# A transformer block on one core: two weight slabs get their own place, some scalings may run on GpSimd, and the instruction order is planned anew

## The chip, the core and the metric

One core of one Trainium2 chip runs the whole kernel. The core has a matrix engine (TensorE, PE in the profile), a vector engine (VectorE, DVE), a scalar engine (ScalarE, ACT), a general engine (GpSimd, POOL) and a synchronising engine (SyncE, SP), which here only issues DMA transfers. Each engine runs its own list of instructions in order; semaphores hold an instruction back until what it needs is there. The metric is the device time of one launch in microseconds (us). Before the change it is 1142.18 us, the median of three runs (1142.15 to 1142.33).

## What is computed

The input is x with 2048 tokens of 1024 numbers, in bfloat16. A conditioning vector c gives six vectors of 1024 numbers: `mod = silu(c) @ w_mod`, split into sa, ca, ga, sb, cb, gb.

1. `h = layernorm(x) * (1 + ca) + sa`, then attention with 32 heads of width 32. The heads have their own queries (`h @ wq`) but share one key (`h @ wk`) and one value (`h @ wv`). Then `x = x + ga * (attention @ wo)`.
2. `h = layernorm(x) * (1 + cb) + sb`, then a gated feed-forward layer of inner width 3584: `silu(h @ w1) * (h @ w3)`, times w2. Then `x = x + gb * (that)`.

## The kernel before

**Work.** The 2048 tokens are eight blocks of 256. Keys and values are made for all tokens at the start. Then attention goes block by block: for each block eight groups of four heads, and for each group eight *steps*. In a step (`s_exp`, line 834) PE computes the scores of 256 keys against 256 queries for four heads (8 matmuls with 32 rows each, into tile S), and ACT takes the exponential of them in two instructions of 128x1024 (into tile U). There are 512 steps in all, 64 for each block, numbered here 0 to 511. The feed-forward work of block n runs between the steps of block n+1: the projection by wo and the second layer norm (`wo`, line 928), 14 slabs of w1 and w3 (`slab`, line 985: 32 matmuls of 256 columns each), and four quarters of w2 (`quarter`, line 1022: 56 such matmuls). The last block's feed-forward work has nothing beside it and forms a tail. Besides these, `av` (line 865) computes probabilities times values and, with the sums of pairs that DVE makes (`pairs`, line 854, tile PS), the softmax denominators.

**Setup.** At the start x arrives in pieces; each tile of 128 tokens is normalised (`lnt1`, line 640: statistics on DVE, the reciprocal root on POOL, the normalising on ACT or DVE), transposed on PE into HT, and copied out of the PSUM buffer by ACT or DVE. `mod_cols` (line 673) computes sa and ca from two pieces of w_mod for each; `scale0` (line 689) multiplies the first 256 columns of wq by (1 + ca), in eight instructions that may run on DVE or POOL. The first step needs sa, because the key and query biases come from it (`k_bias`, line 703). The other four vectors come from `mod_chunk` (line 793), whose weights go through two places called WMB, inside the tile W2S.

**Second norm.** For blocks 1 to 6 the normalised tokens are transposed by two DMA transfers, and eight DVE instructions of 128x256 (one for each 128 features, cc = 0 to 7) multiply by (1 + cb) and add sb. PE's first slab matmuls read these pieces in the order of cc.

**Weight slabs.** Each slab of w1 and w3 (two transfers of 512 KB, `slab_dma`, line 970) goes to one of three places in turn: two in W13, where wq lies until the last query projection has read it, and one in HT, where the transposed tokens lie until then. W2S holds two quarters of w2; before that it holds x tiles 6 to 15 and the WMB places.

**Order.** No order is written out by hand. A planner (`Placer`, line 194) runs when the kernel is built. Every operation has a duration that the planner is told, a due time `vt`, and an engine or a choice of engines. `choose` (line 284) takes, among the operations that could start about now, the one with the least due time. `PLAN` (line 115) has an entry for every 16 steps: how far from the earliest start it may look, some switches, and an offset of the due time for each kind of operation and engine ("slab/pe": -74). Another PLAN therefore gives another order on each engine. POOL operations are given a longer duration where the planner believes that DVE holds them up. In the profile all recorded instructions have line 22, so they are told apart by tiles.

Of the kernel before, what the change touches and what calls it, by code (L numbers as in the profile page):

```python
# [6 lines left out]
ALU = mybir.AluOpType  # L7
# [35 lines left out]
class Graph:  # L43
# [63 lines left out]
    def alias(self, new, old):  # L107
# [5 lines left out]


PLAN = [
    (0.0, 0.12, 0.2, 1, 0.7,
     {"wo/pe": -19, "mc/pe": 25, "slab/dve": -28, "ln/dve": -40, "k/pe": 5, "mod/pe": 114, "mc/dve": 1}),
    (0.0, 0.12, 0.1, 1, 1.3, {"mc/pe": 27, "q/dve": -2, "ln/pe": 6, "ln/act": 32, "v/pe": 15, "mod/pe": 18}),
    (0.0, 0.12, 0.1, 1, 0.9,
     {"mc/pe": 27, "slab/act": -5, "q/dve": -2, "ln/pe": 6, "ln/act": 32, "v/pe": 15, "mod/pe": 18}),  # L120
    (0.0, 0.12, 0.1, 1, 0.9,
     {"q/pe": -119, "mc/pe": 27, "slab/act": -5, "q/dve": -2, "ln/pe": 6, "ln/act": 32, "v/pe": 15, "mod/pe": 18,
      "kb/pe": -44, "mc/dve": -51}),
    (0.0, 0.16, 0.2, 1, 2.6,
     {"slab/pe": -74, "q/pe": 2, "av/dve": 20, "slab/dve": 32, "slab/act": -7, "q/dve": -2, "mc/dve": 6}),
    (0.0, 0.16, 0.2, 1, 1.6,
     {"slab/pe": -74, "q/pe": 2, "av/dve": 20, "slab/dve": 32, "slab/act": -7, "q/dve": -2, "mc/dve": 6}),
    (0.0, 0.16, 0.2, 1, 1.3,
     {"slab/pe": -74, "q/pe": 2, "av/dve": 20, "slab/dve": 32, "slab/act": -7, "q/dve": -2, "mc/dve": 6}),
    (0.0, 0.13, 0.2, 1, 1.3,  # L130
     {"slab/pe": -74, "q/pe": 2, "av/dve": 20, "slab/dve": 32, "slab/act": -7, "wo/dve": 106, "q/dve": -2,
      "mc/dve": 6}),
    (0.0, 0.13, 0.2, 1, 1.3,
     {"slab/pe": -74, "q/pe": 2, "pair/dve": 22, "av/dve": 20, "slab/dve": 49, "slab/act": -7, "wo/dve": 106,
      "q/dve": -2, "mc/dve": 6}),
    (0.0, 0.11, 0.0, 1, 2.4, {"wo/pe": 4, "slab/pe": 107, "quarter/pe": -2, "q/pe": -26, "an/dve": 4, "q/dve": -119}),
    (0.0, 0.11, 0.02, 1, 2.6,
     {"wo/pe": 4, "slab/pe": 107, "quarter/pe": -2, "q/pe": -26, "an/dve": 4, "q/dve": -119}),
    (0.0, 0.11, 0.02, 1, 2.6,
     {"wo/pe": 4, "slab/pe": 107, "quarter/pe": -2, "q/pe": -26, "an/dve": 4, "q/dve": -119}),  # L140
    (0.0, 0.11, 0.2, 1, 2.6,
     {"wo/pe": 135, "quarter/pe": 20, "mc/pe": -8, "pair/dve": 119, "av/dve": -14, "an/dve": 72,
      "quarter/dve": -26, "wo/dve": 65, "q/dve": -66}),
    (0.0, 0.11, 0.2, 1, 1.4, {"wo/pe": -20, "slab/pe": 107, "q/pe": -26, "an/dve": 54, "q/dve": -119}),
    (0.0, 0.11, 0.02, 1, 3.1,
     {"wo/pe": -20, "q/pe": -26, "mc/pe": -3, "av/dve": 8, "an/dve": 54, "slab/dve": 29, "q/dve": -119}),
    (0.0, 0.11, 0.05, 0, 2.3,
     {"av/pe": -15, "q/pe": -9, "mc/pe": 109, "pair/dve": -1, "an/dve": 4, "slab/act": 15, "q/dve": 7,
      "mc/dve": 6}),
    (0.0, 0.11, 0.2, 1, 2.4,  # L150
     {"wo/pe": 17, "quarter/pe": -15, "mc/pe": -8, "pair/dve": -39, "av/dve": 1, "an/dve": 72,
      "quarter/dve": -26, "wo/dve": 65, "q/dve": -72}),
    (0.0, 0.12, 0.2, 1, 1.3, {"slab/pe": -12, "av/dve": 57}),
    (0.0, 0.11, 0.2, 1, 2.9,
     {"av/pe": -12, "wo/pe": -19, "slab/pe": -9, "quarter/pe": -39, "pair/dve": -2, "an/dve": -117,
      "quarter/dve": -16, "q/dve": -105}),
    (0.0, 0.11, 0.2, 1, 1.9,
     {"av/pe": -12, "wo/pe": -19, "slab/pe": -9, "quarter/pe": -39, "pair/dve": -2, "an/dve": -117,
      "quarter/dve": -16, "q/dve": -105}),
    (0.0, 0.11, 0.2, 1, 1.9,  # L160
     {"av/pe": -12, "wo/pe": -19, "slab/pe": -9, "quarter/pe": -39, "pair/dve": -2, "an/dve": -117,
      "quarter/dve": -16, "q/dve": -105}),
    (0.0, 0.11, 0.2, 0, 0.7,
     {"av/pe": -12, "wo/pe": -19, "slab/pe": -9, "quarter/pe": -39, "pair/dve": -2, "an/dve": -143,
      "quarter/dve": -16, "q/dve": -105}),
    (0.0, 0.11, 0.05, 1, 3.1,
     {"wo/pe": -17, "mc/pe": -8, "av/dve": 1, "an/dve": 47, "slab/act": 11, "quarter/dve": -26, "wo/dve": 86}),
    (0.0, 0.11, 0.05, 1, 3.1,
     {"wo/pe": -17, "mc/pe": -8, "av/dve": 1, "an/dve": 47, "slab/act": 11, "quarter/dve": -26, "wo/dve": 86}),
    (0.0, 0.11, 0.05, 1, 3.1,  # L170
     {"wo/pe": -17, "mc/pe": -8, "av/dve": 1, "an/dve": 47, "slab/act": 11, "quarter/dve": -26, "wo/dve": 86}),
    (0.0, 0.14, 0.2, 0, 0.1, {"slab/pe": -12, "pair/dve": -20, "av/dve": -18, "slab/dve": -24}),
    (0.0, 0.11, 0.05, 0, 3.3,
     {"wo/pe": -17, "mc/pe": -8, "pair/dve": 43, "av/dve": 14, "slab/act": 9, "quarter/dve": -26}),
    (0.0, 0.11, 0.05, 0, 3.3,
     {"wo/pe": -17, "mc/pe": -8, "pair/dve": 43, "av/dve": 14, "slab/act": 9, "quarter/dve": -26}),
    (0.0, 0.11, 0.2, 1, 1.4,
     {"av/pe": -15, "quarter/pe": -3, "q/pe": -9, "mc/pe": 33, "pair/dve": -16, "av/dve": -5, "an/dve": 18,
      "quarter/dve": -37, "q/dve": 7, "mc/dve": 6}),
    (0.0, 0.11, 0.2, 1, 1.4,  # L180
     {"quarter/pe": -3, "q/pe": -9, "mc/pe": 33, "av/dve": -5, "an/dve": 18, "quarter/dve": 74, "q/dve": 7,
      "mc/dve": 6}),
    (0.0, 0.11, 0.0, 1, 1.4,
     {"quarter/pe": -3, "q/pe": -9, "mc/pe": 33, "av/dve": -5, "an/dve": 18, "quarter/dve": 74, "q/dve": 7,
      "mc/dve": 6}),
    (0.0, 0.11, 0.05, 0, 4.1,
     {"wo/pe": -17, "slab/pe": -70, "mc/pe": -8, "pair/dve": 43, "av/dve": 14, "slab/dve": 97, "slab/act": 9,
      "quarter/dve": -26}),
    (0.0, 0.11, 0.2, 0, 3.3,
     {"slab/pe": -13, "quarter/pe": 27, "mc/pe": 61, "slab/dve": -16, "quarter/dve": 6, "wo/dve": 2}),  # L190
]


# [257 lines left out]
def build(nc, x_in, wq_in, wk_in, wv_in, wo_in, w1_in, w3_in, w2_in, c_in, wmod_in, out, S, D, F):  # L451
    G = Graph(nc)
    op = G.op
    NC = D // P
# [72 lines left out]
    O2B = HTf[:, o:o + 1024].rearrange("p (s t d) -> p s t d", s=2, t=2)  # L527
    o += 1024
    assert o <= NC * S
    W13SL = [W13[:, 0], W13[:, 1], W13C]  # L530
    WQ = W13[:].rearrange("p a b c f -> p (a b c f)").rearrange("p (c f) -> p c f", c=NC)
    WM0 = Uf[:, 0:NC * 2048].rearrange("p (c f) -> p c f", c=NC)
    WMB = [W2f[:, 10 * D:10 * D + NC * 512].rearrange("p (c f) -> p c f", c=NC),
# [52 lines left out]
        dma("sp", dst, x2[tt0 * P:(tt0 + cnt) * P, :].rearrange("(t p) d -> p t d", p=P), ("XL", tt0),  # L586
            cnt * P * D * 2, writes=keys, vt=vt, bw=FAST)

    WSPL = (0, 4, NC)

    def wm_dma(fld, h, vt):
        c0, c1 = WSPL[h:h + 2]
# [326 lines left out]
    def h2t(n):  # L919
        return H20 if n == 0 else QT[:, n - 1, :, :]  # L920

    def h2k(n):
        return [("H20", cc) for cc in range(NC)] if n == 0 else [("QT", n - 1, cc) for cc in range(NC)]

    def xk(n, t, qs=range(4)):
        return [("X", n % NX, t, q) for q in qs]

    def wo(n, vt):
        G.tag = "wo"
        for t in range(2):  # L930
# [26 lines left out]
        for hh in range(2):  # L957
            s = Sess()
# [4 lines left out]
            for k in range(4):  # L963
# [21 lines left out]
    def slab(n, s, vt):  # L985
        G.tag = "slab"
        slab_dma(n, s, vt - 12)
        r = (n * NSLAB + s) % NW
        g = (n * NSLAB + s) % 2
        ss = [Sess(), Sess()]  # L990
        for m in range(2):
# [213 lines left out]
```

## Time and profile before

| what | value |
|---|---|
| median of 3 runs | 1142.18 us (1142.15 to 1142.33) |
| profiled execution, its own time | 1142.53 us |
| its span (first to last instruction) | 1140.7 us |
| granted TensorE clock | 1.00 |
| PE busy, matmul instructions | 1115.7 us, 15538 |
| ACT busy | 1024.3 us |
| DVE busy | 953.9 us |
| POOL busy | 38.3 us |
| first matmul of step 0 | 30.49 us |
| first matmul of step 511 | 1041.95 us |

Times within the profile count from the start of the span. A busy PE is not the same as a PE at its best: matmuls overlap, and the profile models their ends. The starts of the instructions are what the readings below use. A step's time is the time from the first score matmul of a step to that of the next.

### The profile page before, as it was taken

What the parts mean: (1) busy time and instruction counts of PE and PEld (TensorE: products, weight loads), DVE (VectorE), ACT (ScalarE), POOL (GpSimd) and SP (SyncE); (2) the same over time, 40 slices, a digit from 0 to 9 for tenths busy, and PEclk for the clock granted to TensorE, in tenths of its full rate; (3) what the DMA queues carried; (4) which work ended last, traced back from release to release, by engine and by line L of the source; (5) the groups of instructions that cost most, each with busy time, mean ns of one, the idle gap of its engine ahead of it and who ended that gap; (6) DMA issues with size and microseconds to landing.
All of it is one profiled execution on the core that took longest, in us unless ns stands there. A gap on an engine that the chain in (4) does not pass through costs nothing.

```text
span 1140.7 us, 34695 instructions
## 1 busy us (share of the span) xinstructions
PE 1115.7 (98%) x15538; PEld 756.8 (66%) x15568; DVE 953.9 (84%) x1557; ACT 1024.3 (90%) x1161; POOL 38.3 (3%) x83
## 2 busy tenths in 40 slices
PE   8999999999999999999999999999999999999998
PEld 7644556666577756776567656776577656776887
DVE  7888899998888888888979799888978988888442
ACT  5999999999999999999999999999999999996110
POOL 4100000000000000000000010000100000000000
PEclk9999999999999999999999999999999999999999
DMA  9500379665596668665696659675686658667793
GB/s 345 179 2 1 113 222 245 181 187 155 132 264 194 172 163 221 191 196 154 145 253 196 173 143 236 192 204 131 156 249 192 174 140 231 194 188 202 222 291 118
DMA packets 374291, 209.45 MB, mean 184 GB/s; under 512 B 17536, under 2 KB 365952, under 8 KB 374144
## 3 DMA queue, kind: packets, MB, share of 16 engines
q1 hardware_dynamic: 373712, 207.11, 65.2%
q8 instruction: 122, 2.00, 0.8%
q14 instruction: 25, 0.20, 0.1%
q10 hardware_dynamic: 432, 0.13, 0.0%
HBM read 199.89 MB, written 4.19 MB: 179 GB/s over the span
## 4 chain that ended last, share of the span: by engine, by line
ACT 48%; PE 41%; DVE 8%; DMA 2%; issue 1%; SPq 0%; POOL 0%; DVEq 0%
ACT U L22 44%; PE PB L22 29%; PE S L22 12%; DVE PS L22 4%; ACT HT L22 4%; DVE QT L22 1%; DMA W<-in_A_wq_dram 1%; DVE HT L22 1%; DVE RB L22 1%; DVE X L22 0%; DMA QT<-XNB 0%; SPq L22 0%; DVE ST L22 0%; DVE XNB L22 0%; DVE RC L22 0%
## 5 line engine op out<-in xcount | busy, mean ns | idle before, releaser
L22 ACT ACTIVATE U<-S 128x1024 bf16<-128x1024 f32 x1024 | 962.8, 1105 | 15.7 <-PE S L22 7.7
L22 DVE TENSOR_TENSOR PS<-U 128x2048 bf16<-128x2048 bf16 x256 | 309.1, 1213 | 21.3 <-ACT U L22 19.2
L22 DVE TENSOR_TENSOR PS<-PS 128x1024 bf16<-128x1024 bf16 x368 | 248.9, 685 | 4.0
L22 PE MATMUL PB<-QT,W 128*128 128x256 bf16 x1856 | 230.6, 273 | 0.9 <-DVE RB L22 0.4
L22 PE MATMUL S<-QT,KT 32*128 32x256 bf16 x4096 | 203.4, 273 | 7.8 <-ACT U L22 5.5
L22 PEld LDWEIGHTS PB<-QT,W 128*128 128x128 bf16 x1856 | 169.9, 98 | 49.3 <-issue 26.8
L22 PE MATMUL PB<-W2S,HT 128*128 128x256 bf16 x1512 | 189.8, 273 | 0.0
L22 PEld LDWEIGHTS PB<-W2S,HT 128*128 128x128 bf16 x1512 | 136.9, 98 | 43.8 <-issue 27.2
L22 PEld LDWEIGHTS S<-QT,KT 32*128 32x128 bf16 x4096 | 60.7, 92 | 134.8 <-ACT U L22 122.4
L22 PE MATMUL PB<-U,V 128*32 128x256 bf16 x4032 | 125.6, 273 | 1.6 <-DVE HT L22 1.0
L22 PE MATMUL PB<-QT,HT 128*128 128x256 bf16 x960 | 120.6, 273 | 0.6 <-DVE HT L22 0.3
L22 PEld LDWEIGHTS PB<-U,V 128*32 128x32 bf16 x4032 | 99.7, 96 | 23.4 <-issue 10.8
L22 ACT ACTIVATE HT<-PB 128x512 bf16<-128x512 f32 (+1 forms) x110 | 76.4, 696 | 32.7 <-PE PB L22 32.6
L22 PEld LDWEIGHTS PB<-QT,HT 128*128 128x128 bf16 x960 | 87.7, 98 | 25.8 <-issue 14.0
L22 PE MATMUL PB<-HT,W 128*128 128x256 bf16 (+1 forms) x561 | 98.5, 316 | 2.4 <-issue 1.6
L22 DVE SCALAR_TENSOR_TENSOR HT<-HT,PB 128x512 bf16<-128x512 bf16 x102 | 69.4, 681 | 31.8 <-ACT HT L22 30.9
L22 DVE TENSOR_TENSOR HT<-HT,PB 128x512 bf16<-128x512 bf16 x102 | 69.5, 682 | 15.0 <-PE PB L22 13.2
L22 PEld LDWEIGHTS PB<-HT,W 128*128 128x128 bf16 x576 | 50.2, 97 | 37.0 <-issue 13.9
L22 PE MATMUL PB<-WO,QT 128*128 128x512 bf16 x217 | 54.0, 380 | 1.8 <-issue 1.3
L22 DVE STREAM_TRANSPOSE RB<-PB 128x256 f32<-128x256 f32 x63 | 28.2, 447 | 29.6 <-PE PB L22 29.4
L22 POOL TENSOR_SCALAR RS<-MV 128x1 f32<-128x1 f32 x32 | 11.3, 354 | 1015.4 <-DVE MV L22 1010.4
L22 DVE COPY RB<-PB 128x256 f32<-128x256 f32 x63 | 26.4, 419 | 18.5 <-PE PB L22 18.5
(112 smaller groups left out, 648.9 us busy)
## 6 DMA issues: line engine op xcount, KB each, us to landing
W<-in_B_w_dram SPq DMA_DIRECT2D x150, 512.0 KB, 4.9
W2S<-in_B_w_dram SPq DMA_DIRECT2D x28, 1792.0 KB, 8.3
HT<-in_B_w_dram SPq DMA_DIRECT2D x74, 512.0 KB, 4.9
W2S<-in_w_mod_dram SPq DMA_DIRECT2D x8, 1024.0 KB, 6.8
X<-in_A_x_dram SPq DMA_DIRECT2D x8, 512.0 KB, 6.3
U<-in_w_mod_dram SPq DMA_DIRECT2D x4, 1024.0 KB, 11.4
out_dram<-X SPq DMA_DIRECT2D x7, 512.0 KB, 7.9
U<-in_B_w_dram SPq DMA_DIRECT2D x1, 3584.0 KB, 14.0
```

Source lines behind the costliest of these rows:

```text
L22: return getattr(e, call[0])(*call[1], **call[2])
```

## The change

Four things are changed in the text of the kernel.

- Slabs 0 and 1 of block 0 get places of their own (numbers 3 and 4) inside W2S: slab 0 where x tiles 10 to 13 lay, slab 1 where x tiles 6 to 9 and then one WMB place lay. All other slabs keep the place that they had. The first two quarters of w2 now must wait until these slabs have been read.
- Each vector of w_mod that `mod_cols` needs is loaded as 6 and 2 pieces of the inner dimension in place of 4 and 4.
- The second norm's scaling of blocks 1 to 6 is planned with 0.258 us in place of 0.17, and may be placed on POOL, with 0.8 us.
- PLAN has other entries, so that all engines' orders can differ everywhere.

```diff
 PLAN = [
-    (0.0, 0.12, 0.2, 1, 0.7,
-     {"wo/pe": -19, "mc/pe": 25, "slab/dve": -28, "ln/dve": -40, "k/pe": 5, "mod/pe": 114, "mc/dve": 1}),
...
+    (0.0, 0.2, 0.2, 0, 1.3, {"mc/pe": -16, "pair/dve": -90, "av/dve": -32, "k/pe": -82, "k/dve": 48, "mod/pe": 53}),
+    (0.0, 0.16, 0.2, 1, 1.5,
+     {"mc/pe": 77, "pair/dve": -90, "q/dve": -23, "ln/pe": -133, "k/pe": -188, "k/dve": 48, "v/pe": 86,
+      "mod/pe": 53, "kb/pe": 104}),
...
 ]
...
-    W13SL = [W13[:, 0], W13[:, 1], W13C]
+    W13SL = [W13[:, 0], W13[:, 1], W13C] + [
+        W2f[:, k * D:(k + 4) * D].rearrange("p (m c f) -> p m c f", m=2, c=NC) for k in (4, 0)]
+    NE = 2
...
-    WSPL = (0, 4, NC)
+    WSPL = (0, 6, NC)
...
-                   0.17, reads=[("h2r", n, 0), ("h2r", n, 1), ("MODC", 3, cc // 4), ("MODC", 2, cc // 4)],
-                   writes=[h2k(n)[cc]], vt=vt)
+                   0.258, reads=[("h2r", n, 0), ("h2r", n, 1), ("MODC", 3, cc // 4), ("MODC", 2, cc // 4)],
+                   writes=[h2k(n)[cc]], vt=vt, alts=[("pool", lambda cc=cc: [lambda e: e.tensor_scalar(
+                       h2t(n)[:, cc, :], h2t(n)[:, cc, :], MODC[:, 3, cc:cc + 1], MODC[:, 2, cc:cc + 1], ALU.mult,
+                       ALU.add)], 0.8)] if POOLH else [])
...
+    def wslot(n, s):
+        return NW + s if n == 0 and s < NE else (n * NSLAB + s) % NW
+
     def slab_dma(n, s, vt):
-        r = (n * NSLAB + s) % NW
+        r = wslot(n, s)
...
-    G.alias([("W2S", r) for r in range(2)], [("XS", tt) for tt in range(6, NTT)] + [("WMB", 0), ("WMB", 1)])
+    G.alias([("W13", NW, m) for m in range(2)], [("XS", tt) for tt in range(10, 14)])
+    G.alias([("W13", NW + 1, m) for m in range(2)], [("XS", tt) for tt in range(6, 10)] + [("WMB", 1)])
...
+        if n == 0:
+            G.alias([("W2S", r) for r in range(2)], [("XS", tt) for tt in range(6, NTT)] + [("WMB", 0), ("WMB", 1)] +
+                    [("W13", NW + k, m) for k in range(NE) for m in range(2)])
```

The built programs show what the planner makes of it. PE's list has the same 15568 matmuls in both. A matmul list changes its kind (scores; column-tiled av matmuls; all others) 1115 times before and 1102 times after. In the second norm of each of blocks 1 to 6, the pieces cc = 1 and cc = 5 go to POOL and the other six stay on DVE; of the eight scalings in `scale0`, three are on POOL and five on DVE (before two and six).

More of the change, by code (lines that the diff above doesn't have):

```diff
@@ L115 @@
 PLAN = [
-    (0.0, 0.12, 0.2, 1, 0.7,
-     {"wo/pe": -19, "mc/pe": 25, "slab/dve": -28, "ln/dve": -40, "k/pe": 5, "mod/pe": 114, "mc/dve": 1}),
[L118 to L140, printed above, removed]
@@ L141 @@
-    (0.0, 0.11, 0.2, 1, 2.6,
[L142 to L190, printed above, removed]
+    (0.0, 0.2, 0.2, 0, 1.3, {"mc/pe": -16, "pair/dve": -90, "av/dve": -32, "k/pe": -82, "k/dve": 48, "mod/pe": 53}),
+    (0.0, 0.16, 0.2, 1, 1.5,
+     {"mc/pe": 77, "pair/dve": -90, "q/dve": -23, "ln/pe": -133, "k/pe": -188, "k/dve": 48, "v/pe": 86,
+      "mod/pe": 53, "kb/pe": 104}),
@@ new lines @@
+    (0.0, 0.11, 0.2, 0, 2.2,
+     {"wo/pe": 106, "q/pe": -78, "mc/pe": 6, "q/dve": 38, "ln/pe": -118, "ln/dve": 4, "mod/pe": -24}),
+    (0.0, 0.12, 0.2, 0, 0.7, {"wo/pe": 106, "q/pe": -78, "q/dve": 38, "ln/pe": -118, "ln/dve": 4}),
+    (0.2, 0.13, 0.2, 1, 0.8, {"q/pe": 47, "mc/pe": 46, "ln/act": -12, "k/pe": 22}),
+    (0.0, 0.13, 0.2, 1, 1.7, {"q/pe": 47, "mc/pe": 46, "pair/dve": -11, "av/dve": 4, "ln/act": -12, "k/pe": 22}),
+    (0.0, 0.11, 0.2, 1, 1.4, {"q/pe": 47, "mc/pe": 46, "av/dve": 4, "ln/act": -12, "k/pe": 22}),
@@ new lines @@
+    (0.0, 0.11, 0.2, 1, 1.9, {"q/pe": -13, "mc/pe": 46, "av/dve": 4, "ln/act": -12, "k/pe": 22}),
+    (0.0, 0.11, 0.2, 1, 3.9,
+     {"wo/pe": 35, "q/pe": -13, "mc/pe": 46, "av/dve": 4, "slab/dve": 15, "ln/act": -12, "k/pe": 22}),
+    (0.0, 0.11, 0.2, 1, 1.4, {"av/dve": -11, "an/dve": 55, "slab/dve": 1, "q/dve": 9}),
+    (0.0, 0.11, 0.1, 0, 2.4,
+     {"wo/pe": 14, "slab/pe": 12, "quarter/pe": 3, "q/pe": -6, "av/dve": 18, "an/dve": 69, "slab/act": -1,
+      "quarter/dve": -7}),
+    (0.0, 0.11, 0.02, 0, 2.9, {}),
@@ new lines @@
+    (0.0, 0.11, 0.2, 0, 2.9, {"wo/pe": 46, "an/dve": 55, "slab/dve": -89, "q/dve": 67}),
+    (0.0, 0.11, 0.2, 1, 1.3, {"wo/pe": -13, "pair/dve": 6, "an/dve": 55, "slab/dve": -89, "q/dve": 67}),
+    (0.0, 0.11, 0.1, 1, 2.7,
+     {"slab/pe": -132, "q/pe": 47, "mc/pe": 46, "pair/dve": -13, "av/dve": 23, "slab/dve": -39, "slab/act": -20,
+      "quarter/dve": -47, "ln/act": -12, "k/pe": 22}),
+    (0.0, 0.11, 0.1, 1, 2.3,
+     {"slab/pe": -132, "q/pe": 47, "mc/pe": 46, "pair/dve": -13, "av/dve": -84, "slab/act": -20,
+      "quarter/dve": -47, "ln/act": -12, "k/pe": 22}),
@@ new lines @@
+    (0.0, 0.11, 0.2, 1, 4.1,
+     {"wo/pe": 138, "slab/pe": -132, "quarter/pe": 13, "q/pe": 47, "mc/pe": 46, "pair/dve": -13, "av/dve": -83,
+      "slab/dve": -39, "slab/act": -20, "quarter/dve": -47, "ln/act": -12, "k/pe": 22}),
+    (0.0, 0.11, 0.2, 1, 1.3,
+     {"slab/pe": -124, "q/pe": 47, "mc/pe": 46, "pair/dve": -24, "av/dve": -89, "an/dve": -26, "slab/dve": -39,
+      "slab/act": -20, "ln/act": -12, "k/pe": 22}),
+    (0.0, 0.11, 0.05, 1, 3.7,
+     {"wo/pe": -5, "quarter/pe": 48, "pair/dve": -3, "av/dve": -2, "slab/act": -7, "wo/dve": 20}),
@@ new lines @@
+    (0.0, 0.11, 0.05, 1, 3.7,
+     {"wo/pe": -5, "quarter/pe": 48, "pair/dve": -3, "av/dve": -2, "slab/act": -7, "wo/dve": 20}),
+    (0.0, 0.11, 0.2, 1, 2.6,
+     {"wo/pe": 112, "slab/pe": -124, "quarter/pe": 26, "q/pe": 20, "mc/pe": 46, "pair/dve": 13, "av/dve": -89,
+      "an/dve": -26, "slab/dve": -39, "slab/act": -20, "quarter/dve": 35, "wo/dve": -2, "ln/act": -12,
+      "k/pe": 22}),
+    (0.0, 0.11, 0.2, 1, 1.3,
+     {"slab/pe": -124, "quarter/pe": 26, "q/pe": 52, "mc/pe": 46, "pair/dve": 13, "av/dve": -72, "an/dve": -26,
+      "slab/dve": -39, "slab/act": -20, "quarter/dve": 35, "wo/dve": -6, "ln/act": -12, "k/pe": 22}),
@@ new lines @@
+    (0.0, 0.11, 0.05, 1, 2.6,
+     {"slab/pe": -124, "quarter/pe": 26, "q/pe": 20, "mc/pe": 46, "av/dve": -89, "slab/dve": -39,
+      "slab/act": -20, "quarter/dve": 35, "ln/act": -12, "k/pe": 22}),
+    (0.0, 0.11, 0.05, 1, 1.4,
+     {"slab/pe": -124, "quarter/pe": 26, "q/pe": 20, "mc/pe": 5, "av/dve": -89, "slab/act": -20,
+      "quarter/dve": 35, "ln/act": -12, "k/pe": 22}),
+    (0.0, 0.11, 0.2, 0, 1.6, {"wo/pe": 74, "pair/dve": 40, "av/dve": -2, "an/dve": 55, "slab/dve": -102, "q/dve": 6}),
@@ new lines @@
+    (0.0, 0.11, 0.2, 1, 1.4, {"wo/pe": -13, "pair/dve": 40, "av/dve": -2, "an/dve": 55, "slab/dve": -88}),
+    (0.0, 0.11, 0.05, 1, 1.9,
+     {"slab/pe": -124, "quarter/pe": -21, "q/pe": 20, "mc/pe": 46, "pair/dve": 43, "av/dve": -89,
+      "slab/dve": -39, "slab/act": -20, "quarter/dve": 35, "ln/act": -12, "k/pe": 22}),
+    (0.0, 0.11, 0.05, 1, 1.9,
+     {"slab/pe": -124, "quarter/pe": -21, "q/pe": 20, "mc/pe": 46, "pair/dve": 43, "av/dve": -89,
+      "slab/act": -20, "quarter/dve": 35, "ln/act": -12, "k/pe": 22}),
@@ new lines @@
+    (0.0, 0.11, 0.2, 0, 3.4, {"wo/pe": 61, "q/pe": -20, "pair/dve": 3, "slab/dve": -23, "wo/dve": 33}),
+    (0.0, 0.11, 0.2, 1, 1.4, {"wo/pe": -5, "quarter/pe": 48, "pair/dve": -20, "av/dve": -27, "slab/act": -7}),
+    (0.0, 0.11, 0.05, 0, 2.1,
+     {"slab/pe": -124, "quarter/pe": -21, "q/pe": 20, "mc/pe": 46, "pair/dve": 43, "av/dve": -89,
+      "slab/dve": -39, "slab/act": -20, "quarter/dve": 35, "q/dve": -75, "ln/act": -12, "k/pe": 22}),
+    (0.0, 0.11, 0.05, 0, 4.0,
+     {"slab/pe": -124, "quarter/pe": -21, "q/pe": 20, "mc/pe": 46, "pair/dve": 43, "av/dve": -89,
+      "slab/act": -20, "quarter/dve": 35, "q/dve": -75, "ln/act": -12, "k/pe": 22}),
@@ L191 @@
+    (0.0, 0.11, 0.2, 0, 3.7,
+     {"wo/pe": -4, "slab/pe": -43, "q/pe": 20, "mc/pe": 46, "pair/dve": 43, "av/dve": 55, "slab/dve": -39,
+      "slab/act": -20, "quarter/dve": 35, "q/dve": -75, "ln/act": -12, "k/pe": 22}),
 ]
@@ L926, in xk @@
         return [("X", n % NX, t, q) for q in qs]
+    POOLH = True
     def wo(n, vt):
@@ L987, in slab @@
         slab_dma(n, s, vt - 12)
-        r = (n * NSLAB + s) % NW
+        r = wslot(n, s)
         g = (n * NSLAB + s) % 2
```

## The prediction

> **What bounds the kernel now.** I read the page's engine shares first, then the busy time of each stage, then the order of time around single steps.
>
> ```profile
> PE 1115.7 (98%) x15538; PEld 756.8 (66%) x15568; DVE 953.9 (84%) x1557; ACT 1024.3 (90%) x1161; POOL 38.3 (3%) x83
> ACT 48%; PE 41%; DVE 8%; DMA 2%; issue 1%; SPq 0%; POOL 0%; DVEq 0%
> ```
>
> PE and ACT share the chain that ends last. The busy times of the stages, cut at the starts of steps 128, 192, 256 and so on, show why:
>
> ```profile
> 278.50:406.77 128.27, 127.56 (x1807) 86.71 (x1808) 111.14 (x178) 124.79 (x143) 1.91 (x4) 1.00 0.70 188
> 406.77:533.82 127.05, 125.84 (x1790) 85.30 (x1793) 111.31 (x178) 124.99 (x143) 2.74 (x4) 1.00 0.69 187
> 533.82:664.06 130.24, 128.76 (x1808) 86.64 (x1810) 112.03 (x177) 125.14 (x143) 1.91 (x4) 1.00 0.70 189
> 1041.95:1137.54 95.59, 95.54 (x910) 82.25 (x910) 41.47 (x72) 11.06 (x17) 1.58 (x4) 1.00 0.81 228
> ```
>
> The columns are stretch, length, then PE, PEld, DVE, ACT and POOL busy, clock, DMA share and GB/s. With the last stage ACT is done and PE alone works 95 us; so every matmul done earlier shortens the end, and PE's list sets the time. How a step is made up is seen here:
>
> ```profile
> 428.80 0.40 PE L22 MATMUL S<-QT,KT 32*128 32x256 bf16 x8
> 429.13 1.48 PE L22 MATMUL PB<-W2S,HT 128*128 128x256 bf16 x12
> 430.55 0.40 PE L22 MATMUL S<-QT,KT 32*128 32x256 bf16 x8
> ```
>
> From 428.80 to 430.55 a step with 12 matmuls of 256 columns took 1.75 us. A fit over the undisturbed ones of the steps from 120 on gives their prices: scores 0.227, a 256-column matmul 0.108, a 512-column one 0.213, a column-tiled one 0.027, and about 0.115 for each change of kind. With these the 1107 us from step 0 to the last matmul hold 1093 us of PE work and changes of kind and some 14 us of waits. ACT needs 2 x 0.904 a step (0.917 early on), close below.
>
> **Blocks 2 to 7.** PE's order after the change is the same in all six (up to where the last one runs into the tail), and it is the order that block 3 (steps 192 to 255) has now in 62 of 64 steps, block 7 in 61. So they are priced like for like. From step 128 to the last matmul is 859.04 us now (278.50 to 1137.54). Five blocks at block 3's 127.05 and the last one with its tail at 220.26 (917.28 to 1137.54) are 855.51: -3.5 us. Of this 2.3 is PE work that lies earlier or is gone (13 changes of kind fewer, 1.5 us in all), 1.2 are waits.
>
> Block 3 itself contains a wait of 0.65 in step 206 that block 7 has with 0.10 only; there the second DMA transpose came late:
>
> ```profile
> 434.56 2.14 DVE L22 TENSOR_SCALAR QT<-QT,MODC 128x256 bf16<-128x256 bf16 x8 [0.46 <-DMA QT<-XNB]
> ...
> 436.61 0.68 DVE L22 TENSOR_TENSOR HT<-PB,GBR 128x512 bf16<-128x512 f32 x1
> ```
>
> Whether it comes late in all five blocks is open: 0 to -0.5 each, I take -0.25, so -1.2.
>
> **Scalings on POOL.** In six blocks cc = 1 and cc = 5 move from DVE to POOL. The nearest row is the same form, two scalings beside six on DVE:
>
> ```profile
> 17.87 1.95 POOL L22 TENSOR_SCALAR PS<-W,MODC 128x256 bf16<-128x256 bf16 x2 [2.20 <-DMA W<-in_A_wq_dram]
> ...
> 426.95 0.55 POOL L22 TENSOR_SCALAR RS<-MV 128x1 f32<-128x1 f32 x1 [3.43 <-DVE MV L22]
> 427.58 1.40 POOL L22 TENSOR_TENSOR RS<-RS,NH 128x1 f32<-128x1 f32 x1
> ```
>
> That is 0.98 each. DVE's starts there lie 0.42 apart where a POOL instruction begins and 0.20 elsewhere, so each costs DVE 0.22. From DVE's start T, POOL starts 0.14 later and has cc 1 at T+1.2, cc 5 at T+2.2 with its semaphore; DVE ends its six at T+2.0 (now eight at T+2.14). PE needs cc 0 and 1, then 2 and 3, then scores, then 4 and 5. Now the last pair starts at T+2.33 (436.89); afterwards cc 5 at 2.2 and two matmuls of 0.22 give T+2.42. So +0.1 a block, +0.6. Bounds: if the two cost DVE nothing and POOL kept pace, -0.3 a block; if POOL is stretched 2.5-fold, as the second row is (0.57 uncontended, 1.40 beside a DVE pair sum of 1.22), cc 5 comes at T+5.1: +2.9 a block. The first row has this shape and this neighbour, so I stay by it. What DVE saves is 0.1 us, so nothing behind it gains.
>
> **Block 1 (steps 64 to 127).** Its PE work rises by 1.0 us (the earlier work named above). Its waits are 4.1 now, about 2.2 of them where an av group is split over steps; afterwards each group of 64 stands whole in one step, as in block 3, where that costs 0.11. Five of those: -1.7, so -0.7; bounds -2 and +1, and I take -0.5 since ACT is at 124.4 of 124.9 us here.
>
> **The setup.** Here the change costs. The last pieces of sa's weights land at 23.13 and 25.84 now, 1 MB each 2.71. With 6 and 2 parts the first lands at 20.42 + 1.5 x 2.71 = 24.5. And POOL now does three scalings, to 20.8 in place of 19.83, ahead of the roots of tiles 6 and 7, whose transposes PE's list has before all 64 matmuls for sa:
>
> ```profile
> 23.50 2.08 PE L22 MATMUL PB<-SCC,U 128*128 128x64 bf16 x32
> 25.42 0.68 PE L22 MATMUL PB<-IDENT,XNB 128*128 128x128 bf16 x8
> 25.93 2.08 PE L22 MATMUL PB<-SCC,U 128*128 128x64 bf16 x32
> 27.84 0.67 PE L22 MATMUL PB<-IDENT,PS 128*128 128x128 bf16 x8
> 28.35 0.41 PE L22 MATMUL PB<-SAB,PS 128*128 128x64 bf16 x8
> ```
>
> Tile 7 is normalised by 24.7 and transposed by 25.3; 64 matmuls of 0.061 end at 29.2, now 27.84: +1.4. DVE copies two more transposed tiles out (0.6 each) ahead of sa, which it has at about 29.7, now 28.14. I take +1.5 for step 0: 32.0 in place of 30.49. Bounds: by the landing alone 24.5 + 3.9 = 28.4, +0.5; with DVE in full +1.7.
>
> **Block 0 after its first step.** To step 9 ACT sets the pace now: 18 exponentials of 0.917, five copies of 0.92 and one key eviction of 0.48 make 21.6, and the trace has 21.8. Afterwards there are three copies and three evictions: -0.9. DVE gets two copies more and two evictions fewer (1.2 - 0.8), and is busy 3.55 of 4 there: +0.4 if it decides. I take -0.4 in between (-1.1 to +0.6). The rest of the block has the same exponentials and within 0.2 us the same PE work.
>
> **The places of their own.** I cost these at nothing. Slab 0 starts at step 77 (178.0) in both orders; its weights are there at 160.8 already, and what it waits for is the second norm. No wait for a slab transfer is in the table of waits. The new wait, w2's two quarters behind slab 1's last matmul, sits on SP's queue at about 187 in place of 171; behind it are the reloads for slab 5 and on. The two took to 187.1, 16 us; so they end at 203, the first reload at 205 (such landings lie 1.7 apart), slab 5 begins at about 206. The cover is 1 us; without it, each us of lateness is one us, once. The quarters themselves are needed at 250.
>
> **Sum.** -3.5 - 1.2 + 0.6 - 0.5 + 1.5 - 0.4 = -3.5 us. Against the profiled execution (1142.53, span 1140.7) that is 1139.0; the median of the runs lies 0.35 lower: 1138.7 us.
>
> **Rivals.** A measurement of this kernel tells 0.2%, 2.3 us, from no change. (a) No change that counts: the setup's loss stands, and the waits of block 1 and the late transposes stay as they are: -3.5 + 0.6 + 1.0 + 1.5 - 0.4 = -0.8, 1141.4. For it: those gains are my readings of waits, not of work. Against: PE's identical blocks. It decides from 1.2 us of lost gain on. 0.31. (b) Slower: POOL's instruction holds DVE back for its whole 1.0 us, not for 0.22. Then DVE's six end at T+3.6, the last pair starts 1.3 later than now, and six blocks lose 7.6 in place of 0.6: 1145.7. It is slower from 0.95 more a block on. For it: the stretched row at 427.58 shows that the two engines do hinder each other. Against: 17.87 shows 0.22. 0.08. (c) The change of places does what it says: with weights there earlier, block 0's slabs run with no wait at all and the 2.9 us of waits from step 80 to 127 go: 1.2 more than I took, 1137.5; the absence of DMA waits speaks against it. 0.05.
>
> [...]
>
> **Numbers.** My forecast, faster by 1.5 to 6 us, 0.56, of which a tenth falls within 0.2%; (a) 0.31, of which a tenth is slower, with a setup that costs still more; (b) 0.08; (c) 0.05. So faster 0.55, same 0.34, slower 0.11. The range: downward the bounds of block 1 and the transposes (-1.5 and -1.3), not all at once, 1136.0; upward to (a) and the setup's and DVE's upper bounds, 1142.6.
>
> **What would show it.** Step 0 at 32.0; step 128 at 279.1 (278.50 + 1.5 - 0.4 - 0.5); each block from 2 to 6 at 126.5 to 127.2; step 448 at 913.6 (now 917.28). Twelve POOL scalings of 1.0 us. If step 0 is at 31.0 or earlier, the setup is misjudged; if blocks take over 128 us, POOL's scalings are; if slab 5's matmuls wait for DMA, the places are.

## The result, and the profile after

The changed kernel takes 1136.96 us, the median of five runs (1136.06 to 1137.61); five runs of the kernel before beside it took 1142.15 us (1141.78 to 1142.33). The ratio is 0.9955, with a 95% interval of 0.9941 to 0.9970: faster by 5.2 us. The forecast was 1138.7. The profiled execution of the changed kernel took 1137.61 us, with a span of 1135.8; that is 4.9 us less than the one before (1142.53), where the forecast had 3.5 less.

The engine shares and the chain on the page after:

```profile
PE 1117.0 (98%) x15568; PEld 760.0 (67%) x15568; DVE 955.5 (84%) x1546; ACT 1020.8 (90%) x1159; POOL 53.3 (5%) x96
PE 67%; ACT 26%; DVE 4%; DMA 2%; issue 0%; SPq 0%; POOL 0%; DVEq 0%; POOLq 0%
```

PE is as busy as before; of the chain it now holds 67% where it held 41%, and ACT 26% where it held 48%. The stages after, cut at the starts of steps 64, 128, 192, 256, 320 and 511, show where PE stopped waiting. The columns are stretch, length, then PE, PEld, DVE, ACT and POOL busy, clock, DMA share, GB/s; the lines are block 1, blocks 2 to 4, and the last stage:

```profile
156.09:281.41 125.32, 121.30 (x1822) 80.55 (x1823) 114.82 (x189) 124.67 (x143) 2.55 (x4) 1.00 0.70 190
281.41:407.56 126.15, 125.71 (x1792) 85.56 (x1793) 110.72 (x174) 124.79 (x143) 5.03 (x6) 1.00 0.70 189
407.56:534.27 126.71, 125.85 (x1792) 85.40 (x1792) 111.15 (x175) 124.78 (x143) 3.95 (x6) 1.00 0.69 188
534.27:660.42 126.15, 125.70 (x1792) 85.57 (x1792) 111.21 (x175) 124.79 (x143) 5.05 (x6) 1.00 0.70 189
1037.03:1132.51 95.48, 95.48 (x909) 82.21 (x909) 41.13 (x72) 11.06 (x17) 1.59 (x4) 1.00 0.82 228
```

Blocks 2 and 4 to 6 take the same 126.15 us to the hundredth; block 3 is the odd one, with 126.71. The tail is as long as before (95.48; 95.59 in the stage shown before). How a step is made up has not changed: twelve 256-column matmuls stand between scores at 682.46 and 684.20, 1.74 us, where it was 1.75.

```profile
682.46 0.40 PE L22 MATMUL S<-QT,KT 32*128 32x256 bf16 x8
682.79 1.48 PE L22 MATMUL PB<-W2S,HT 128*128 128x256 bf16 x12
684.20 0.40 PE L22 MATMUL S<-QT,KT 32*128 32x256 bf16 x8
```

A fit over the undisturbed steps of the changed kernel gives nearly the prices of the prediction's fit (0.110 us for a 256-column matmul, 0.113 for a change of kind), so these are used for both kernels, and what is left of a step's time beyond them is taken as wait. In the table a length is the time from the first weight load of one step's scores to that of another; PE work is the matmuls and changes of kind in it at those prices, so work and waits are estimates and only the lengths are measured.

| stretch | length before | after | difference | PE work, difference | waits before | after |
|---|---|---|---|---|---|---|
| start to step 0 | 30.49 | 33.29 | +2.80 | | | |
| block 0 | 123.08 | 122.80 | -0.28 | -0.17 | 1.8 | 1.7 |
| block 1 | 124.93 | 125.32 | +0.39 | +0.98 | 4.1 | 3.6 |
| blocks 2 to 6 | 638.78 | 631.31 | -7.47 | -2.31 | 9.1 | 3.9 |
| block 7 to step 511 | 124.67 | 124.31 | -0.36 | 0 | | |
| sum, to step 511 | 1041.95 | 1037.03 | -4.92 | | | |

The setup cost more than forecast (+1.5), block 1 lost 0.4 where 0.5 was to be gained, and blocks 2 to 7 gave more (-7.8 against -4.1 with POOL's part). The second norm that runs in block 3's steps, which the prediction was priced from, reads as follows after, and below it the one in block 5's steps, on DVE and POOL:

```profile
435.28 1.87 DVE L22 TENSOR_SCALAR QT<-QT,MODC 128x256 bf16<-128x256 bf16 x6 [0.40 <-DMA QT<-XNB]
435.35 1.21 POOL L22 TENSOR_SCALAR QT<-QT,MODC 128x256 bf16<-128x256 bf16 x2 [5.59 <-DMA QT<-XNB]
...
686.53 1.22 DVE L22 TENSOR_TENSOR PS<-U 128x2048 bf16<-128x2048 bf16 x1
687.66 1.78 DVE L22 TENSOR_SCALAR QT<-QT,MODC 128x256 bf16<-128x256 bf16 x6
689.36 0.68 DVE L22 TENSOR_TENSOR HT<-PB,GBR 128x512 bf16<-128x512 f32 x1
...
686.55 2.31 POOL L22 TENSOR_SCALAR QT<-QT,MODC 128x256 bf16<-128x256 bf16 x2 [3.92 <-DMA QT<-XNB]
```

DVE's scalings now take 1.78 us where they took 2.14. In block 5 the transposed tokens are there before DVE has finished its pair sum. POOL starts at 686.55, DVE only at 687.66. POOL's first scaling lasts 1.72 us there and its second 0.60; in block 3, where no pair sum runs beside them, the two take 0.6 each. So POOL is held until the pair sum ends, and then both engines are at their scalings at once: eight scalings on DVE alone start 0.257 us apart (2.14 in all, the last one 0.34), six beside POOL's 0.288 (1.78) or 0.306 (1.87). One of POOL's costs DVE 0.08 to 0.12 us. The single instructions of the trace show how: under each of POOL's twelve scalings one on DVE is longer, 0.42 to 0.51 us in place of 0.34, and it ends 0.08 us after POOL's, as if held until then. The next one on DVE begins within 5 ns of POOL's second scaling, takes the usual 0.33 and ends 0.26 before it. So each engine does hold the other up here, but DVE only for the rest of one scaling.

By this reading POOL's 1.72 us beside the pair sum are 1.12 of waiting and its usual 0.60, an estimate from the two durations. For the scalings the trace shows less: one on DVE seems held until POOL is done, but another runs unheld within POOL's 0.60. What makes the difference no run shows.

The wait for POOL's scalings in the setup, first on PE before, then on POOL and PE after, to set beside the rows of the prediction:

```profile
19.97 1.03 PE L22 MATMUL S<-HT,PS 128*128 128x256 bf16 x8 [1.58 <-POOL PS L22]
...
18.21 2.85 POOL L22 TENSOR_SCALAR PS<-W,MODC 128x256 bf16<-128x256 bf16 x3 [1.49 <-DMA W<-in_A_wq_dram]
...
17.36 1.04 PE L22 MATMUL S<-HT,PS 128*128 128x256 bf16 x8
18.23 0.38 PE L22 MATMUL S<-IDENT 128*128 128x256 bf16 x2
21.12 1.39 PE L22 MATMUL S<-HT,PS 128*128 128x256 bf16 x8 [2.50 <-POOL PS L22]
22.30 0.42 PE L22 MATMUL S<-IDENT 128*128 128x256 bf16 x1
22.52 1.06 PE L22 MATMUL S<-IDENT,PS 128*128 128x128 bf16 x8
23.37 2.10 PE L22 MATMUL S<-IDENT 128*128 128x256 bf16 x10
...
26.75 4.04 PE L22 MATMUL PB<-SCC,U 128*128 128x64 bf16 x64
30.63 0.69 PE L22 MATMUL PB<-IDENT,PS 128*128 128x128 bf16 x8
31.15 0.41 PE L22 MATMUL PB<-SAB,PS 128*128 128x64 bf16 x8
```

The ten fillers at 23.37 (IDENT by IDENT, whose result nobody uses) say that something else happens here: 0.21 us each, where in other runs they take 0.12. Two stretches, the second at the half clock and the first as long ahead of it, in the columns of the stages, show what:

```profile
18.27:21.68 3.41, 0.91 (x10) 0.57 (x8) 3.34 (x11) 1.45 (x2) 3.24 (x5) 1.00 1.05 387
21.68:25.09 3.41, 3.41 (x23) 2.63 (x21) 1.92 (x5) 2.48 (x2) 1.68 (x5) 0.50 1.06 383
```

PE was busy for 0.91 of 3.41 us, and then its granted clock was 0.50 for 3.41 us. Before, the wait at this place was 1.58 us and the clock stayed whole. The 64 matmuls for sa begin at 26.75; their second group of 32 began at 25.93 before.

### The profile page after: what moved, and what is told of

It is laid out like the page before. It is cut to its first block, busy times and chain, and to the rows that moved or that the text cites. A ratio compares the mean times of both kernels' runs of the same rounds, so it can differ in the third digit from the quotient of the medians.

```text
span 1135.8 us, 34733 instructions
## 1 busy us (share of the span) xinstructions
PE 1117.0 (98%) x15568; PEld 760.0 (67%) x15568; DVE 955.5 (84%) x1546; ACT 1020.8 (90%) x1159; POOL 53.3 (5%) x96
## 4 chain that ended last, share of the span: by engine, by line
PE 67%; ACT 26%; DVE 4%; DMA 2%; issue 0%; SPq 0%; POOL 0%; DVEq 0%; POOLq 0%
PE PB L22 51%; ACT U L22 25%; PE S L22 16%; DVE PS L22 2%; DMA W<-in_A_wq_dram 1%; ACT HT L22 1%; DVE HT L22 1%; DMA QT<-XNB 0%; DVE X L22 0%; DVE RB L22 0%; SPq L22 0%; DVE QT L22 0%; POOL PS L22 0%; DVE ST L22 0%; DVE XNB L22 0%
## 5 line engine op out<-in xcount | busy, mean ns | idle before, releaser
L22 PE MATMUL PB<-U,V 128*32 128x256 bf16 x4032 | 123.1, 273 | 0.6 <-DVE HT L22 0.6
L22 PE MATMUL PB<-HT,W 128*128 128x256 bf16 (+1 forms) x512 | 93.7, 324 | 0.6 <-DVE HT L22 0.2
L22 PEld LDWEIGHTS PB<-HT,W 128*128 128x128 bf16 x512 | 44.3, 98 | 36.2 <-issue 12.7
L22 PE MATMUL PB<-WO,QT 128*128 128x512 bf16 x232 | 57.3, 381 | 0.0
L22 PEld LDWEIGHTS PB<-WO,QT 128*128 128x128 bf16 x232 | 19.8, 98 | 25.0 <-issue 7.2
```

The lines of the kernel that those rows point to most:

```text
L22: return getattr(e, call[0])(*call[1], **call[2])
```

## The experiments

In every experiment the planner's search is replaced by the recorded list of what it had chosen (operation, engine, PSUM bank), so that one entry can be altered and all else stays:

```diff
-    choose(): least due time among the operations that can start, guided by PLAN
+    run(): the next entry of ORDER
```

The runs fall into three sessions, each with the kernel before on the same chip: 1142.22 us (1141.74 to 1142.47) beside the first four, 1142.44 (1142.03 to 1143.44) beside the next four, 1142.16 (1141.90 to 1142.72) beside the last two. Ratios are to these.

**The old setup with the new order behind it.** My theory was that the setup's loss comes off one for one.

```diff
-ORDER = after
+ORDER = before up to step 0, then after
-    WSPL = (0, 6, NC)
+    WSPL = (0, 4, NC)
```

> The changed kernel, but everything that stood ahead of step 0's scores in the old order is taken from the old kernel (order, engines, the split 4 and 4). Theory A, that the change loses 2.8 us in its setup (step 0 at 33.29 in place of 30.49) and that this loss goes straight to the end: step 0 at 30.5, 1136.96 - 2.8 = 1134.2 us. Theory B, that the later setup is absorbed where ACT or PE waits anyway: step 0 at 30.5, but 1136.5 to 1137.2 us. Part of what the new order gained after step 0 (ACT has one copy of 0.9 us fewer there) may be lost, which would leave 1134.2 to 1135.1.

Measured: 1135.01 us (1134.66 to 1135.68), ratio 0.9939 [0.9926, 0.9953]; step 0 at 30.22, step 128 at 279.03, step 511 at 1034.09. The order after step 0 is worth 7.2 us, and of this the changed kernel's setup gives back about 2. In the profiled executions step 0 comes 3.07 us earlier than in the changed kernel and step 511 2.94 earlier: the loss goes on to the end, as theory A said (1135.01 is inside the 1134.2 to 1135.1 that it left room for), while 0.7 is lost again in blocks 0 and 1, and 0.6 is won in block 3, where the transposed tokens came in time. The medians differ by less, 1.95, since the profiled execution of the changed kernel was the slowest of its five and that of this run the fastest. This version is faster than both kernels.

**Two scalings of wq on POOL.** The third (c = 7) goes back to DVE.

```diff
-    scale0, c = 7: pool
+    scale0, c = 7: dve
```

> The changed kernel in its own order, but the third of POOL's first-weight scalings is done by DVE behind its own five, so POOL has two and DVE six, as in the old kernel. Theory A1, that this third instruction is the root of the setup's loss: the query matmuls start about 1.0 us earlier (at 20.1 in place of 21.12), PE's idle time ahead of them falls from 2.50 to 1.5, the granted clock does not drop to 0.5 after it (it did from 21.68 to 25.09), and step 0 comes at 31.3 to 31.8: 1135.0 to 1135.6 us. Theory A2, that the order of the transposes ahead of sa's 64 matmuls and the copies on DVE are the root: step 0 stays at 32.5 or later, 1136.3 us or more.

Measured: 1135.44 us (1135.08 to 1135.83), ratio 0.9941 [0.9928, 0.9953]; step 0 at 31.12, PE's wait ahead of the query matmuls 1.38 us, clock 1.00 in the profiled execution; one of the five runs had a mean clock of 0.998. This is what theory A1 forecast, but not all of it is the third scaling: wq's first piece came 0.6 us earlier than in the changed kernel's profile.

**The pieces of w_mod 4 and 4 again.**

```diff
-    WSPL = (0, 6, NC)
+    WSPL = (0, 4, NC)
```

> The changed kernel in its own order, with the vectors' weights loaded as 4 and 4 pieces again. The old trace has the parts of sa's weights at 23.13 and 25.84; the new one has them at 24.82 and 26.18 and its 64 matmuls at 26.75, behind both. Theory A (the split costs nothing in this order, since PE comes later than both parts): within 0.5 us of the changed kernel, 1136.5 to 1137.5. Theory C (the later landing of the first part holds the setup back, as the prediction's lower bound of 0.5 us has it): 1136.0 to 1136.5. If ca's second half of 32 matmuls, behind its landing at 13.6, now ends 0.9 later, nothing should follow, because the scalings that need it wait for a landing at 18.05.

Measured: 1137.11 us (1135.99 to 1138.37), ratio 0.9956 [0.9943, 0.9968]; step 0 at 32.81, with PE's wait of 2.56 us and the clock at 0.50 after it. So the pieces cost nothing that can be measured (theory A); the 0.5 us that I had as the lower bound for step 0, "by the landing alone", is not seen: step 0 is 0.48 us earlier than in the changed kernel's profile, but there wq's first piece had come 0.43 later (POOL's scalings start at 18.21 there, at 17.78 here).

**The old order up to step 128.** This was meant to price blocks 0 and 1.

```diff
-ORDER = after
+ORDER = before up to step 128, then after
-    WSPL = (0, 6, NC)
+    WSPL = (0, 4, NC)
-    NE = 2
+    NE = 0
```

> The old kernel's order, split and places of the slabs up to step 128, and the changed kernel's order from there on. Theory A, that all of the gain lies from step 128 on (there 7.8 us in the profiles, 859.04 against 851.1) and that setup, new places and blocks 0 and 1 only lose (2.9 us by step 128): step 128 at 278.5, 1134.2 to 1134.6 us, faster than both kernels. Theory C, that the slabs' own places help block 1 and the new order has only hidden this behind the setup's loss: slower than the kernel with the old setup alone, by more than 0.5 us. The seam moves 0.8 us of PE work behind step 128, which both theories count the same.

Measured: 1136.69 us (1135.95 to 1137.26), ratio 0.9951 [0.9939, 0.9964]. That missed by 2 us, and by its time alone it would be theory C's. The trace has another reason: up to step 127 it goes like the old kernel (276.55), and then step 127 holds 28 matmuls of w2 where the old kernel has 12. The old order had these 16 (16 x 0.108 = 1.7 us) still to do, and the list puts what the new order has done by then in front of step 128, which starts at 280.42. So at equal work the new order reaches step 128 1.4 us sooner (279.03 in the first run; 0.2 of it is a wait for w2's transfer that only this seam has), although the stretch is 0.8 us longer than in the old kernel. Nine changes of kind fewer in blocks 0 and 1 (278 in place of 287), 1.0 us by the fitted price, are the greater part of it. What the places do for block 1 is tested below.

**The second norm's scalings back on DVE.** All 12 of POOL's, each between its neighbours.

```diff
-    second norm of blocks 1 to 6, cc = 1 and cc = 5: pool
+    second norm of blocks 1 to 6, cc = 1 and cc = 5: dve
```

> The twelve second-norm scalings that the change puts on POOL go back to DVE, each between its neighbours; every other list is the changed kernel's. Theory A (POOL starts with the DMA transpose, beside DVE's pair sum, so that DVE is done with its six 0.36 us earlier than with eight): 0.36 us come back in each of six blocks, step 128 to the last matmul 853.3 us instead of 851.1, time 1139.2 (1138.5 to 1140.5). Rival B (the new order of PE alone took the waits away, the scalings only moved): time 1136.5 to 1137.6, step 128 to the end 851.0 to 851.5.

Measured: 1137.23 us (1137.20 to 1139.58), ratio 0.9961 [0.9948, 0.9973]. By its time alone this would be rival B's. But its setup went better than in the changed kernel's profile (step 0 at 30.84, see below), and what was in question lies behind: from step 128 to step 511 it takes 757.66 us, the changed kernel 755.62. That is 2.04 us, 0.34 for each of six blocks, as theory A said. The run "Shared places again" of the same session, whose start was as good (31.06), has a median 1.79 us lower. In blocks 2, 4, 5, 6 and 7 the whole 0.36 lies in one step, the eighteenth of the block. In block 5, on PE:

```profile
692.19 0.40 PE L22 MATMUL S<-QT,KT 32*128 32x256 bf16 x8 [0.16 <-ACT U L22]
692.94 1.93 PE L22 MATMUL PB<-U,V 128*32 128x256 bf16 x64 [0.35 <-DVE HT L22]
```

and in the changed kernel, same step:

```profile
693.64 0.40 PE L22 MATMUL S<-QT,KT 32*128 32x256 bf16 x8 [0.16 <-ACT U L22]
694.02 1.93 PE L22 MATMUL PB<-U,V 128*32 128x256 bf16 x64
```

The wait is not on a scaling. It is on HT, DVE's work on a slab's result, that stands behind the scalings and the pair sums in DVE's list and reads a PSUM buffer; the next av group is held up by it. That HT sets this buffer free for av is my reading of the releaser in the row. Eight scalings in place of six put HT 0.36 us later (7.12 us after the start of the pair sum ahead of the scalings, in the changed kernel 6.76). The kernel before shows the same wait in step 209, two steps after the last row that I had read:

```profile
441.28 1.93 PE L22 MATMUL PB<-U,V 128*32 128x256 bf16 x64 [0.20 <-DVE HT L22]
```

**The old kernel with POOL's scalings.** The same thing from the other side.

```diff
-ORDER = before
+ORDER = before, second norm of blocks 1 to 6, cc = 1 and cc = 5: pool
```

> The old kernel with one thing changed: cc = 1 and cc = 5 of the second norm's scalings in blocks 1 to 6 run on POOL. Theory A: DVE is done 0.36 us earlier in six blocks; the old kernel has 0.2 to 0.7 us of waits on the scalings in each, 3.0 in all, so 1.5 to 2.5 of these go: 1139.7 to 1140.7. Rival B (order, not POOL): 1141.7 to 1142.5. Rival C (POOL holds DVE back): above 1142.7.

Measured: 1140.64 us (1139.81 to 1141.27, eleven runs), ratio 0.9983 [0.9974, 0.9992]: 1.8 us faster. From step 128 to step 511 it takes 761.54 us, the kernel before 763.45. The two experiments agree: 2 us are POOL's scalings, with either order. In block 3 the wait on HT is gone:

```profile
440.40 1.93 PE L22 MATMUL PB<-U,V 128*32 128x256 bf16 x64
```

But of the 0.40 us that this block gains only 0.08 lie in that step. 0.33 lie in step 206, where PE waits for the scalings themselves, behind the late transpose. So where the tokens come late the consumer gains, and where they come in time it is the HT behind it.

**Shared places again.** Slabs 0 and 1 of block 0 are loaded into the shared places behind block 0's queries.

```diff
-    NE = 2
+    NE = 0
-ORDER = after
+ORDER = after, with the transfers of block 0's slabs 0 to 4 and w2's first quarters at the old kernel's points of SP's list
```

> Slabs 0 and 1 of block 0 go back to the shared places and are loaded when these are free, behind block 0's queries; w2's first quarters start at the old kernel's point of SP's list; the order of PE, DVE, ACT and POOL is the changed kernel's. Theory A (the places were worth nothing, since slab 0 waits for the second norm): 1136.4 to 1137.6, no wait for a slab's transfer. Rival C (early weights are what lets block 0's slabs run without waits): slabs 0 to 2 wait for their transfers around step 77, 1137.8 or more, the waits of steps 64 to 127 rise from 3.6 to 4.5 or more.

Measured: 1135.44 us (1134.79 to 1135.57), ratio 0.9937 [0.9924, 0.9949]. Steps 64 to 127 take 125.32 us, the same as in the changed kernel, and the waits in them are 3.55 us in both. The places are worth nothing, as theory A said. The run is faster than its 1136.4 and than the changed kernel's median; in the profiled execution that is the setup again, with step 0 at 31.06.

**A third scaling on POOL,** on top of the fastest version so far.

```diff
-ORDER = before up to step 0, then after
+ORDER = before up to step 0, then after, second norm of blocks 1 to 6, cc = 3: pool
-    WSPL = (0, 6, NC)
+    WSPL = (0, 4, NC)
```

> Old setup and new order after it (the fastest version so far, 1135.01), with a third scaling of each second norm, cc = 3, on POOL as well. If DVE's end sets PE's remaining wait of 0.35 us a block: up to 0.35 less in six blocks, 1132.9 to 1134.3. If POOL's own last one (cc = 5, now third, done about 0.6 to 1.0 us later than now, at T+1.8 to 2.2 after DVE's start) sets it: 1135.0 to 1137.

Measured: 1134.46 us (1134.31 to 1135.71), ratio 0.9932 [0.9919, 0.9944]. From step 128 to step 511 it takes 754.72 us, against 755.06 in the first run: 0.06 a block, so neither expectation holds. Little was left to gain: from the start of that step's scores to av it is 0.75 us with eight scalings on DVE, 0.38 with six (the rows above) and 0.33 here with five (691.89 to 692.22). The 0.16 on ACT, as in the row at 693.64, is still there. It is the fastest version, though its interval overlaps that of the first run. Its profiled execution, the slowest of the five (1135.71), shows the half clock at another place, in step 77, which starts at 177.95 (the columns as above):

```profile
174.70:178.10 3.40, 1.72 (x32) 1.14 (x32) 3.40 (x10) 3.40 (x5) 0.00 (x0) 1.00 0.35 97
178.10:181.50 3.40, 3.40 (x28) 1.73 (x21) 3.30 (x7) 2.81 (x4) 0.00 (x0) 0.51 0.02 5
```

**The changed kernel once more, and its idle time filled.** By now the setup needed a test of its own. Across the runs the profiled executions had this:

| run | first scaling on POOL starts | scalings on POOL | PE's wait ahead of the queries | clock behind it | step 0 |
|---|---|---|---|---|---|
| before | 17.87 | 2 | 1.58 | 1.00 | 30.49 |
| old setup, new order | 17.56 | 2 | 1.24 | 1.00 | 30.22 |
| two on POOL | 17.59 | 2 | 1.38 | 1.00 | 31.12 |
| pieces 4 and 4 | 17.78 | 3 | 2.56 | 0.50 | 32.81 |
| after | 18.21 | 3 | 2.50 | 0.50 | 33.29 |
| scalings on DVE | 16.50 | 3 | 1.06 | 1.00 | 30.84 |
| shared places | 16.64 | 3 | 1.18 | 1.00 | 31.06 |

The other three runs so far have the old setup, with two scalings on POOL, and a whole clock there too. The first scaling starts when wq's first piece has landed, and that differs from run to run with the same list of transfers. In these executions the clock halves only where the piece is late and a third scaling follows; with two scalings it stayed whole behind a landing as late as 17.87. The next run is the recorded list as it is, with no edit; the one after it moves fillers into the wait.

> The changed kernel once more, nothing edited, beside the next run on the same chip. In the runs so far the clock fell to half when wq's first piece landed late (POOL's scalings start at 17.8 to 18.2 us, PE idle about 2.5 us ahead of the query matmuls) and stayed whole when it landed early (16.5 to 16.6, idle 1.1 to 1.2). So a run is at 1136.9 to 1137.6 with a mean clock of 0.998, or at 1135.0 to 1136.1 with 1.00; on the earlier chip it was four of the first kind and one of the second.

Measured: 1136.24 us (1134.95 to 1137.57), ratio 0.9952 [0.9939, 0.9966]: three runs with a mean clock of 1.00 at 1134.95 to 1136.24, two with 0.998 at 1137.36 and 1137.57. In the profiled execution wq is early (POOL starts at 16.76) and step 0 at 30.88.

```diff
-    PE: 2 fillers, query matmuls, 1 filler, transposes, 10 fillers
+    PE: 15 fillers, query matmuls, transposes
```

> The changed kernel with PE's 13 filler matmuls (IDENT by IDENT, result unused) that stand behind the first query matmuls moved ahead of them, into the wait for POOL's three scalings: no work more or less, three scalings still on POOL. Theory A (PE's idle 2.5 us is what halves the clock): the idle time there falls to 1 us or less, the clock stays at 1.00 in all runs, step 0 at 30.7 to 31.3, time 1135.0 to 1135.8 in all five. Rival B (the clock falls for another reason, for instance with the late transfer itself): runs at 1136.9 to 1137.6 with 0.998 remain.

Measured: 1136.29 us (1135.50 to 1136.49), ratio 0.9946 [0.9934, 0.9959]. In its profiled execution wq was late and three scalings were on POOL:

```profile
17.83 2.86 POOL L22 TENSOR_SCALAR PS<-W,MODC 128x256 bf16<-128x256 bf16 x3 [1.11 <-DMA W<-in_A_wq_dram]
```

and on PE:

```profile
18.24 1.80 PE L22 MATMUL S<-IDENT 128*128 128x256 bf16 x15
20.75 1.05 PE L22 MATMUL S<-HT,PS 128*128 128x256 bf16 x8 [0.71 <-POOL PS L22]
```

The clock was 1.00 all through and step 0 came at 31.71, later than the 30.7 to 31.3 of theory A. With the same lateness (17.78) it had been 32.81, and with 18.21 it had been 33.29. So in the profiled executions it is PE's idle time at this place that goes with the half clock, and not the late transfer by itself. That rests on one filled execution, and the times bear it out only in part. None of the five lies at the 1136.9 to 1137.6 of rival B, but four lie above the 1135.8 of theory A, the median is no lower than that of the unedited run beside it (1136.24), and two have a mean clock of 0.998 and 0.997, at 1136.49 and 1136.30. No trace of these two was kept. The stretch before step 77, where another run had its half clock, is one place where this may have been; that was not tried.

## Why the prediction was right, and where it was wrong

The time was inside the range and on the right side, 1.7 us below the forecast. But errors of opposite sign stand behind it: blocks 2 to 7 gave 3.7 us more, the setup cost 1.3 more in the profiled execution, and block 1 came out 0.9 worse. That the total came so close is in part luck.

- **Blocks 2 to 7 like for like, -3.5.** Right. All of them now have PE's work of block 3 to the matmul, and the 2.3 us of PE work that the prediction counted there are the 2.31 of the table (16 matmuls of w2 that lie in block 1 now, and fewer changes of kind).
- **The late transposes, -1.2.** Mis-sized. With the scalings back on DVE, the only difference left at this place, blocks 2, 4, 5 and 6 take 126.50 us and block 3, where the transposed tokens still came late, 127.00; the old block 3 took 127.05. So not late is worth 0.5 to 0.55, the upper bound, in four blocks: about -2.1. In block 3 they came late in some runs (after, 126.71) and not in others (126.15 in the first run); why is open.
- **Scalings on POOL, +0.6.** This step failed, in sign too: -2.0. The prices were wrong: I took 0.98 us for each of POOL's and 0.22 for what it costs DVE, from the setup. Here it is 0.60 and 0.08 to 0.12, so cc = 1 is there at T+0.6 and cc = 5 at T+1.2, not T+1.2 and T+2.2, and DVE is done at T+1.78 in place of T+2.14. That POOL begins when the transfer lands, and not with DVE, adds little, as it is held through the pair sum: in block 3, where both start together, it is T+0.7, T+1.3 and T+1.87. And the sentence "What DVE saves is 0.1 us, so nothing behind it gains" was wrong in both halves: DVE saves 0.36, and in five of the six blocks what gains is just what is behind it, the slab's HT and through it av. The bound of -0.3 a block was the right end.
- **Block 1, -0.5.** Failed: +0.39. Work rose as forecast (+0.98 for +1.0), the waits fell by 0.6, not 1.7. ACT is busy for 124.67 of 125.32 us, 124.45 of 124.93 before; the room under ACT's pace was 0.5 us, and I had spent all of it. That ACT is what kept the waits is argued from this and was not tried; several of the remaining ones are scores behind ACT (U).
- **The setup, +1.5.** Mis-sized in the profiled execution (+2.80), and in a way that no row of before showed. With whole clock it was +0.4 (30.88, wq early) to +1.2 (31.71, wq late, wait filled). What I worked out, POOL's third scaling and then 64 matmuls in a row, is the late case without the clock. The step that it lacks is the granted clock, which halves behind PE's wait of 2.50; by 32.81 - 31.71, at nearly the same lateness, that is worth about 1.1, in two executions that differ in the place of the fillers and in w_mod's pieces as well.
- **Block 0, -0.4, and the places of their own, 0.** Right: -0.28, and the same 125.32 us in block 1 without them. Slab 5's two reloads landed at 207.9 and 209.4, later than forecast (205), and its matmuls begin at 209.76; the cover was thin, but no wait for a slab's transfer is in the profile.
- **The rivals.** (a) is out as a whole, since the waits of the late transposes did go in four of five blocks; but its setup's loss did stand, and block 1's waits went only by a third of what I took. (b) is out: a scaling on POOL costs DVE 0.08 to 0.12 us here, and the old kernel with POOL's scalings is 1.8 us faster, not slower. It is mostly POOL that waits, 1.12 us for DVE's pair sum. (c) is out by the shared places.

## What to carry to other kernels

Where an engine is relieved of work, don't stop at the consumer of that work: follow its list to the next instruction that sets a buffer free, and look for a wait on that. Price a helper engine from a row in the place where it will run: the same form took POOL 0.98 us in the setup and 0.60 here. And a total can hide a part: the setup's luck was as large as the effect to be measured, so compare stretches between the same two steps rather than run times.

## What the runs showed of the hardware that was not expected

- The granted clock of PE fell to 0.50 for 3.41 us after PE had been busy for 0.91 of 3.41 us (one idle stretch of 2.50), after 1.19 of 3.41 us (18.46 to 21.87, with the pieces 4 and 4), and once after 1.72 of 3.40 us with no idle stretch over 0.9. With 1.88 of 3.40 in the same stretch of another run, and with idle times up to 1.58 in the setup, it stayed whole; so it did after 1.63 of 3.41 in the run with the wait filled (20.03 to 23.44), so busy time in such a stretch alone doesn't tell when it falls. In all three cases PE was a quarter to a half busy in the stretch ahead, which is taken about as long as the half clock.
- A scaling of 128x256 on POOL took 0.55 us at the least (in the old kernel with POOL's scalings), 0.60 beside DVE's scalings of the same form in the second norm, 0.95 to 0.98 on average in the setup, and 1.72 where it met a pair sum. Why the setup's take longer than those of the second norm is open.
- The landing of wq's first piece varied by up to 1.7 us (16.50 to 18.21, by POOL's start) with the same list of transfers ahead of it. What sets it was not found.
